# Masks as 32-bit GpSimd products over interleaved row pairs, part of the key writes moved to DMA, eps as a third statistics group, two MLP partial sums in place of three, and a new instruction order

**Chip, cores, metric.** One core of one Trainium2 chip (trn2). The metric is the device time of one execution in microseconds (us); lower is better. Of several runs the median is quoted. The kernel runs on one core, so there is no slower die to compare with; every profiled run of this study is in the fast state, with a mean granted TensorE clock between 0.92 and 1.00.

## The reference

Two identical layers over a 2048 x 512 input: windowed attention, then an MLP that mixes along the sequence. Cut to what matters:

```python
def _A_ref(x, wqkv, wo):                       # B, S, D = 1, 2048, 512
    H = 32; Dh = D // H; W = 256               # 32 heads of 16, window 256
    ...
    scores = jnp.einsum("bhqd,bhkd->bhqk", q, k) * (Dh ** -0.5)
    mask = (idx[:, None] - idx[None, :] >= 0) & (idx[:, None] - idx[None, :] < W)
    p = _softmax(jnp.where(mask[None, None], scores, -1e9), axis=-1)
    ...
def _B_ref(x, w1, b1, w2, b2):                 # F = 1792
    h = _layernorm(x, axis=-1)
    u = _gelu(jnp.einsum("bsd,sf->bdf", h, w1) + b1)
    y = jnp.einsum("bdf,fs->bds", u, w2) + b2
    return y.transpose(0, 2, 1)

for _ in range(2):                             # written out in the original
    x = x + _A_ref(_layernorm(x), A_wqkv, A_wo)
    x = x + _B_ref(_layernorm(x), B_w1, B_b1, B_w2, B_b2)
```

## The kernel before

The kernel first lists all its operations, each with the engines that may run it, and then puts them into the order that a constant, `ORDER`, holds: about 2,500 entries of (next operation, which engine). Every engine runs its own operations in that order and waits on semaphores. So each operation below has a place in an in-order queue, and a change of the place is a change of data, not of code.

Attention works on score units: scores of four head rows for 128 keys and 512 query columns (some have fewer), two PSUM bank pairs, two exps on ScalarE into the bf16 tile `pt`, one or two mask products over the triangular ends of the window, then P V.

```python
for i, ts in enumerate((tA, tB)):
    op("scalar:exp", lambda e, ...: e.activation(
        pt[:, tp.slot, 2 * i:2 * i + 2, 0:cols], pair(ts)[:, :, 0:cols], ACTF.Exp, scale=SMSCALE), ...)
for c0, nc_, w0 in plan[su[0][0]][1]:
    def f_mask(e, ...):
        v = pt[:, tp.slot, :, c0 * 64:c0 * 64 + w]
        msk = ldm[:].rearrange("p a b -> p (a b)")[:, w0 * 64:w0 * 64 + w]
        ...
        return e.tensor_tensor(v, v, msk....to_broadcast([P, 4, w]), op=ALU.mult)
    op("vector:mask", f_mask, ..., alts=[("gpsimd", f_mask, ...)])          # DVE or GpSimd, as the order says
...
# P V reads   rhs=pt[64 * h:64 * h + 64, tp.slot, r, base + c0 * 64:base + (c0 + n) * 64]
```

Keys go through a staging tile into `kbd`, for either half `h` of 16 channels with the other half set to zero, which a product with a 0/1 column (`par`) does:

```python
for h in range(2):
    f_kz = lambda e, h=h: e.tensor_scalar(dst(h), stg[...], par[:, h:h + 1], 0.0, op0=ALU.mult, op1=ALU.add)
    op("gpsimd:kz", f_kz, ..., alts=[("vector", f_kz, ...)])
```

Layer norm takes `bn_stats`, `bn_aggr`, a DVE op for variance plus eps ("var"), a power of -0.5 on GpSimd, and the normalise on DVE. The first MLP product runs in pieces while attention is still going on, and DVE adds each piece to a running sum in SBUF:

```python
PARTS = [[(2, 0, 4), (3, 4, 8), (4, 8, 12)], [(2, 0, 8)]]    # (chunk, first row block, last row block) per layer
```

The softmax here doesn't subtract the row's maximum and nothing guards it: scores larger than these inputs give would overflow.

## Time and profile before

| | kernel before |
|---|---|
| median of 3 runs | 477.62 us (477.6 to 481.74) |
| span of the profiled run, mean granted clock | 476.5 us, 0.988 |
| busy: PE, DVE, ACT, GpSimd (POOL) | 421.0, 368.0, 331.4, 227.6 us |
| first exp starts; last exp of layer 1 and of layer 2 ends | 9.8; 176.0; 394.2 us |
| lengths: attention 1, MLP 1 with attention 2, last MLP | 166.2, 218.2, 82.3 us |

PE is TensorE (PEld its weight loads), DVE VectorE, ACT ScalarE. Busy times say how full an engine is over everything; the three lengths, read off the first and last exp, say where the time goes. The prediction shows the lines behind the table.

### The profile page before, as it was taken

What the parts mean: (1) busy time and instruction counts of PE and PEld (TensorE: products, weight loads), DVE (VectorE), ACT (ScalarE), POOL (GpSimd) and SP (SyncE); (2) the same over time, 40 slices, a digit from 0 to 9 for tenths busy, and PEclk for the clock granted to TensorE, in tenths of its full rate; (3) what the DMA queues carried; (4) which work ended last, traced back from release to release, by engine and by line L of the source; (5) the groups of instructions that cost most, each with busy time, mean ns of one, the idle gap of its engine ahead of it and who ended that gap; (6) DMA issues with size and microseconds to landing.
All of it is one profiled execution on the core that took longest, in us unless ns stands there. A gap on an engine that the chain in (4) does not pass through costs nothing.

```text
span 476.5 us, 14658 instructions
## 1 busy us (share of the span) xinstructions
PE 421.0 (88%) x6355; PEld 199.2 (42%) x6416; DVE 368.0 (77%) x702; ACT 331.4 (70%) x388; POOL 227.6 (48%) x252
## 2 busy tenths in 40 slices
PE   6998887996868688999999998878798999999996
PEld 5855333343323233444554443433333334444442
DVE  7999999989988879726767889998988798630313
ACT  8998988999789780520689989999989992231000
POOL 4677876398477342001046874987755551000000
PEclk9999999999999799999999999999989999999999
DMA  7522604510011317530330310052013136465362
GB/s 220 136 46 62 144 1 36 126 44 3 3 45 34 92 46 227 165 96 11 89 89 14 91 35 3 3 135 46 3 36 89 47 105 183 132 192 142 100 194 71
DMA packets 79392, 39.77 MB, mean 83 GB/s; under 512 B 20960, under 2 KB 79328, under 8 KB 79328
## 3 DMA queue, kind: packets, MB, share of 16 engines
q1 hardware_dynamic: 79328, 38.82, 30.9%
q8 instruction: 51, 0.84, 0.8%
q14 instruction: 13, 0.11, 0.1%
HBM read 33.56 MB, written 2.10 MB: 75 GB/s over the span
## 4 chain that ended last, share of the span: by engine, by line
PE 50%; DVE 30%; ACT 15%; POOL 2%; issue 2%; DMA 0%
PE PS L512 30%; ACT pt L685 14%; DVE pt L695 8%; PE PS L837 7%; PE PS L670 4%; PE PS L607 4%; PE PS L716 4%; DVE rl L736 3%; DVE xh_sb L493 3%; DVE stats L470 2%; DVE x_sb L758 2%; DVE oT L747 1%; DVE vb L618 1%; POOL pt L695 1%; PE PS L514 1%
## 5 line engine op out<-in xcount | busy, mean ns | idle before, releaser
L685 ACT ACTIVATE pt<-PS 128x1024 bf16<-128x1024 f32 (+1 forms) x304 | 283.3, 1043 | 27.1 <-PE PS L670 26.4
L695 POOL TENSOR_TENSOR pt<-pt,ldm 128x256 bf16<-128x256 bf16 (+1 forms) x148 | 147.4, 1006 | 74.3 <-ACT pt L685 62.3
L695 DVE TENSOR_TENSOR pt<-pt,ldm 128x512 bf16<-128x512 bf16 (+1 forms) x124 | 69.7, 569 | 9.1 <-ACT pt L685 7.4
L512 PE MATMUL PS<-xh_sb,w1b 128*128 128x512 bf16 x262 | 69.2, 389 | 7.4 <-issue 2.4
L670 PE MATMUL PS<-qT,kbd 32*128 32x256 bf16 (+4 forms) x1488 | 61.4, 255 | 12.1 <-DVE rl L736 3.6
L512 PE MATMUL PS<-uT,w2b 128*128 128x512 bf16 x268 | 68.4, 379 | 0.9 <-issue 0.6
L486 POOL TENSOR_TENSOR rstd<-rstd,mhalf 128x2 f32<-128x2 f32 (+1 forms) x33 | 23.3, 712 | 78.5 <-DVE rstd L484 77.0
L864 DVE SCALAR_TENSOR_TENSOR x_sb<-PS,b2col,x_sb 128x512 bf16<-128x512 f32 x32 | 23.3, 747 | 47.8 <-PE PS L512 47.7
L716 PE MATMUL PS<-pt,vb 64*32 64x320 bf16 (+4 forms) x2976 | 44.9, 251 | 16.5 <-DVE pt L695 9.0
L512 PE MATMUL PS<-xhT,wqkv 128*128 128x512 bf16 (+1 forms) x218 | 51.6, 364 | 5.3 <-issue 2.2
L670 PEld LDWEIGHTS PS<-qT,kbd 32*128 32x128 bf16 x1488 | 22.1, 93 | 66.9 <-ACT pt L685 40.7
L852 ACT ACTIVATE uT<-rl,b1col 128x512 bf16<-128x512 f32 x28 | 18.3, 712 | 42.5 <-DVE rl L848 42.5
L736 DVE STREAM_TRANSPOSE rl<-PS 128x1024 f32<-128x1024 f32 x32 | 39.7, 1242 | 8.1 <-PE PS L716 7.8
L470 DVE BATCH_NORM_STATS2 stats<-x_sb 128x6 f32<-128x512 bf16 x64 | 42.9, 681 | 3.3 <-DMA x_sb<-in_A_x_dram 2.8
L716 PEld LDWEIGHTS PS<-pt,vb 64*32 64x32 bf16 x2976 | 28.5, 90 | 35.9 <-issue 11.2
L512 PE MATMUL PS<-uT,pt 128*128 128x512 bf16 x165 | 42.2, 379 | 0.2
L512 PEld LDWEIGHTS PS<-xh_sb,w1b 128*128 128x128 bf16 x280 | 23.0, 99 | 39.1 <-issue 11.1
L512 PEld LDWEIGHTS PS<-uT,w2b 128*128 128x128 bf16 x278 | 25.9, 98 | 31.6 <-issue 2.5
L837 PE MATMUL PS<-xh_sb,w1b 128*128 128x512 bf16 x165 | 37.1, 379 | 1.4 <-DVE xh_sb L493 1.2
L493 DVE TENSOR_SCALAR xh_sb<-x_sb,agg,rstd 128x512 bf16<-128x512 bf16 x64 | 34.9, 561 | 2.2 <-POOL rstd L486 2.0
L742 POOL TENSOR_TENSOR ul<-rl,rc 128x512 bf16<-128x512 f32 x23 | 25.8, 1123 | 22.3 <-DVE rc L740 20.5
L607 PE MATMUL PS<-wqkv,xhT 128*64 128x256 bf16 x512 | 34.0, 275 | 1.3 <-DVE rstd L484 1.3
(65 smaller groups left out, 410.3 us busy)
## 6 DMA issues: line engine op xcount, KB each, us to landing
w1b<-in_B_w_dram SPq DMA_DIRECT2D x112, 128.0 KB, 2.7
w2b<-in_B_w_dram SPq DMA_DIRECT2D x70, 128.0 KB, 2.5
pt<-in_B_w_dram SPq DMA_DIRECT2D x42, 128.0 KB, 2.8
out_dram<-x_sb SPq DMA_DIRECT2D x16, 128.0 KB, 2.1
x_sb<-in_A_x_dram SPq DMA_DIRECT2D x3, 512.0 KB, 4.1
wqkv<-in_A_wqkv_dram SPq DMA_DIRECT2D x4, 256.0 KB, 5.1
wqkv<-in_A_wqkv_dram SPq DMA_DIRECT2D x1, 512.0 KB, 6.3
wo_sb<-in_A_wo_dram SPq DMA_DIRECT2D x1, 512.0 KB, 3.8
```

The costliest lines, as they stand in the source:

```text
L470: op("vector:stat", lambda e: e.bn_stats(stats[:, t, :], x_sb[:, t, :]), reads=[f"x{t}"], writes=[f"st{t}"], cost=dve_cost(512), after=lat ...
L486: op("gpsimd:rstd", lambda e: e.tensor_tensor(rstd[:, t0:t1, 0], rstd[:, t0:t1, 0], mhalf[:, 0:1].to_broadcast([P, t1 - t0]), op=ALU.pow), ...
L493: op("vector:xh", lambda e: e.tensor_scalar(xh_sb[:, t, :], x_sb[:, t, :], agg[:, t, 0:1], rstd[:, t, :], op0=ALU.subtract, op1=ALU.mult), ...
L512: return e.matmul(o, lhsT=w, rhs=x, start=start, stop=stop, skip_group_check=True)
L607: last = e.matmul(bank(ft)[64 * j:64 * j + 64, sc * 256:(sc + 1) * 256], lhsT=xhT[:, tx.slot, c, tok:tok + 64], rhs=wqkv[:, c, 1024:1536]. ...
L670: last = e.matmul(bank(tt[r // 2], r % 2)[:, base + c0 * 64:base + (c0 + n) * 64], lhsT=kbd[32 * r:32 * r + 32, tk.slot, o, jj].rearrange( ...
L685: op("scalar:exp", lambda e, ts=ts, tp=tp, i=i, cols=cols: e.activation(pt[:, tp.slot, 2 * i:2 * i + 2, 0:cols], pair(ts)[:, :, 0:cols], A ...
L695: return e.tensor_tensor(v, v, msk.unsqueeze(1).to_broadcast([P, 4, w]), op=ALU.mult)
L716: last = e.matmul(bank(t, h)[32 * r:32 * r + 32, i + q0 * 64:i + (q0 + n) * 64], lhsT=vb[64 * h:64 * h + 64, tk.slot, jj, 4 * o + r, :], r ...
L736: op("vector:od", lambda e, t=tod, tr=tr: e.transpose(rl[:, tr.slot:tr.slot + 2].rearrange("p a b -> p (a b)"), pair(t)), reads=[(tod, i) ...
L742: f_n = lambda e, tr=tr, tl=tl: e.tensor_tensor(ul[:, tl.slot].rearrange("p (q x d) -> p x q d", x=2, d=16), T(tr)[:, :, :, 0:16], R(tl).u ...
L837: last = e.matmul(bank(tu, tt), lhsT=v()[:, sc - b0, k0 + tt * P:k0 + (tt + 1) * P], rhs=xh_sb[:, sc, :], start=(sc == b0), stop=(sc == NT ...
```

## The change

The intent: relieve DVE. Each part takes work from it or from the path that feeds the exps.

1. The probabilities of two score rows are interleaved, so that one int32 holds a pair with the same mask. A mask becomes one GpSimd product over half as many elements; DVE masks are gone.
2. Of 24 key pairs, 14 are written by DMA (eight transfers each) over a `kbd` that was set to zero once.
3. eps enters `bn_aggr` as a third statistics group, so the "var" op goes.
4. The first layer's three partial sums become two.
5. A new order, which also moves some evictions between ACT and DVE.

```diff
-    PARTS = [[(2, 0, 4), (3, 4, 8), (4, 8, 12)], [(2, 0, 8)]]
+    PARTS = [[(2, 0, 4), (4, 4, 12)], [(2, 0, 8)]]
-        ldm = sb("ldm", [P, 4, 64])
+        ldm = sb("ldm", [P, 4, 64], dt.int32)
-        stats = sb("stats", [P, NT, 6], dt.float32)
+        stats = sb("stats", [P, 2, 4, 9], dt.float32)
 ...
+        for i in range(1, 3):
+            op("gpsimd:zk", lambda e, i=i: e.memset(kbd[:, i].bitcast(dt.float32), 0.0), ...)
 ...
+        op("vector", lambda e: e.memset(stats[:, :, :, 6:9], 0.0), writes=["eps0"])
+        for i, c in enumerate((EPS, EPS * EPS / (1.0 + EPS))):
+            op("vector", lambda e, i=i, c=c: e.memset(stats[:, i, :, 8], D * c), ...)
-            op("vector:var", lambda e: e.tensor_scalar(rstd[:, t0:t1, 0], agg[:, t0:t1, 1], a, b, ...), ...)
-            op("gpsimd:rstd", lambda e: e.tensor_tensor(rstd[:, t0:t1, 0], rstd[:, t0:t1, 0], ..., op=ALU.pow), ...)
+            op("gpsimd:rstd", lambda e: e.tensor_tensor(rstd[:, t0:t1, 0], agg[:, t0:t1, 1], ..., op=ALU.pow), ...)
 ...
+        def probs(t):
+            return pt[:, t.slot].rearrange("p a b -> p (a b)").rearrange("p (i c r) -> p i c r", i=2, r=2)
 ...
+                def f_kz(e):
+                    for h in range(2):
+                        for r in range(4):
+                            p = 32 * r + 16 * h
+                            got.append(e.dma_start(kbd[p:p + 16, ...], stg[p:p + 16, ...]))
+                op("sync:kz", f_kz, ..., parts=8, alts=[("gpsimd", f_kz2, 1340), ("vector", f_kz2, ...)])
 ...
-                            pt[:, tp.slot, 2 * i:2 * i + 2, 0:cols], pair(ts)[:, :, 0:cols],
+                            probs(tp)[:, i, 0:cols, :], pair(ts)[:, :, 0:cols].rearrange("p r c -> p c r"),
 ...
+                            v = stepped(probs(tp).bitcast(dt.int32)[:, :, c0:c0 + w, 0], reps, cs)
+                            return e.tensor_tensor(v, v, m, op=ALU.mult)
+                        op("gpsimd:mask", f_mask, ...)
 ...
-                                            rhs=pt[64 * h:64 * h + 64, tp.slot, r, base + c0 * 64:...],
+                                            rhs=probs(tp)[64 * h:64 * h + 64, r // 2, base + c0 * 64:..., r % 2],
```

The rest of the diff is the new `ORDER` constant, a memset of ones over 32-bit words, a merge of two small masks of a unit into one, a factor in the GELU's scale that goes with the third part (`(1.0 + EPS) ** -0.5`, in place of the `1.0 + EPS` in the "var" op), and the bookkeeping of an operation that issues eight transfers.

## The prediction

> **What bounds the kernel now.** I read the page first (busy shares, the 40 slices, the chain by line), then the groups with shapes kept apart, then engine busy time by stage, then the waits of ACT and PE. The page shows no single bound:
>
> ```profile
> PE 421.0 (88%) x6355; PEld 199.2 (42%) x6416; DVE 368.0 (77%) x702; ACT 331.4 (70%) x388; POOL 227.6 (48%) x252
> PE   6998887996868688999999998878798999999996
> DVE  7999999989988879726767889998988798630313
> ACT  8998988999789780520689989999989992231000
> PE 50%; DVE 30%; ACT 15%; POOL 2%; issue 2%; DMA 0%
> ```
>
> The slices show four stages. ACT is high in two blocks, the attention of either layer, and low in two, the two MLPs, where PE alone is at 9. The first and last exp (9.8 and 393 us in the view of their line; in the timeline the first layer's exps stop at 176.0) give the borders, and the busy time of each stage is:
>
> ```profile
> 10.00:176.00 166.00, 137.63 (x2855) 66.68 (x2878) 151.54 (x284) 149.41 (x176) 111.37 (x118) 0.98 0.25 58
> 176.00:248.00 72.00, 69.03 (x528) 33.83 (x517) 50.07 (x105) 25.81 (x36) 10.33 (x14) 1.00 0.42 118
> 248.00:394.00 146.00, 129.29 (x2475) 57.55 (x2497) 127.19 (x236) 136.58 (x152) 99.04 (x106) 0.99 0.21 51
> 394.00:476.50 82.50, 78.26 (x446) 35.55 (x452) 32.56 (x56) 11.85 (x18) 1.79 (x3) 0.99 0.50 144
> ```
>
> Columns after the stretch: PE, PEld, DVE, ACT, POOL, granted clock, DMA share, GB/s. PE is idle only 3.0 and 4.2 us in the MLP stages: they are PE-bound and the change removes no matmul there. In the first attention DVE is 91% busy, ACT 90%, PE 83%; in the second ACT 94%, PE 89%, DVE 87%. So the time to be had is idle time of ACT and PE in the attention stages: ACT 16.6 and 9.4 us, PE 28.4 and 16.7 us. Their waits say why:
>
> ```profile
> ACT pt L685 <- PE PS L670: 26.4, 40, 1.8
> PE PS L716 <- DVE pt L695: 9.0, 13, 2.3
> PE PS L670 <- DVE rl L736: 3.6, 4, 1.1
> ```
>
> ACT's exp waits for scores, in 40 short gaps; PE, in its own order, was held by DVE's mask or by DVE not yet having emptied a PSUM bank. DVE, a fully loaded in-order queue, is the hidden bound of the first attention, ACT close behind.
>
> The parts that the change touches:
>
> ```profile
> L695 POOL TENSOR_TENSOR pt<-pt,ldm 128x512 bf16<-128x512 bf16 x93 | 109.7, 1183 | 50.9 <-ACT pt L685 45.9 <-DVE pt L695 3.3
> L695 DVE TENSOR_TENSOR pt<-pt,ldm 128x512 bf16<-128x512 bf16 x99 | 58.8, 598 | 5.9 <-ACT pt L685 4.2 <-POOL pt L695 1.1
> L695 POOL TENSOR_TENSOR pt<-pt,ldm 128x256 bf16<-128x256 bf16 x55 | 38.6, 707 | 23.4 <-ACT pt L685 16.4 <-DVE pt L695 6.4
> L695 DVE TENSOR_TENSOR pt<-pt,ldm 128x256 bf16<-128x256 bf16 x25 | 11.1, 451 | 3.2 <-ACT pt L685 3.1
> L493 DVE TENSOR_SCALAR xh_sb<-x_sb,agg,rstd x64: 308/406/1319, 5.2 to 407.8; 128x512 bf16<-128x512 bf16 x64
> ```
>
> The last line gives minimum, median and maximum in ns: normalising costs 406 in the median, but 561 in the mean of its group. The tail up to 1319 is not work.
>
> **What the Trainium skill says.** (1) "SBUF — State Buffer", section "Who interferes with whom": GpSimd has only VectorE's second port pair; a VectorE op in a two-port mode, or with two SBUF inputs beside a GpSimd op that reads SBUF, excludes it for the whole instruction. The trace agrees: DVE masks range from 222 to 1845 ns, and at 154.9 us a POOL mask, a DVE mask of 1.41 us and a normalise of 1.14 us follow each other, three times the usual size. (2) "GPSIMD Engine Reference", section 3.1, puts two-input elementwise work at about 2.6 cycles per element, near 2.2 ns. The trace gives (1183 - 707) / 256 = 1.86 ns plus 231 ns fixed, for bf16. That a 32-bit integer multiply costs the same per element no run shows. (3) "SBUF — State Buffer", section "Door 1: The DMA port swizzle", note on cachelines: strides within 16 bytes are free in SBUF (eight bf16), but PSUM lines have 8 bytes and non-contiguous PSUM access slows matmuls. The new layout makes PV read every second bf16 (free by this) and exp read two PSUM banks alternately (not covered; no access of that kind is in the trace). (4) "DMA: Bandwidth & Descriptors", section "Specifications": below 512 B a transfer is not at line rate. The key pieces have 128 B runs, but all kernel loads land in 2 to 3 us here, and the DMA share in attention is 0.25.
>
> **The change, part by part.** The order string is data in the diff; read against the list of operations it has 2,457 entries for 2,531 (33 variance ops, 24 second key halves, 14 partial sums and 8 merged masks fewer, 5 set-up ops more), and it names the engine of each.
>
> Masks: all on POOL, pairs of rows as one int32. Before, 192 masks of 512, 80 of 256, 2 of 1536 and 2 of 512 are 122,880 elements; now 61,440 in 268 ops: 61,440 x 1.86 ns + 268 x 231 ns = 114 + 62 = 176 us on POOL, against 152.5 there before; DVE loses 58.8 + 11.1 + 1.7 = 71.6 us.
> Variance: 33 DVE ops, 7.1 us, go; eps enters the aggregation as a third group. It also takes one hop out of each normalise chain.
> Partial sums: 14 DVE adds of 673 ns, 9.4 us, go. But 56 matmuls (12 us at the 0.216 us between matmuls that the long MLP runs show) leave the fourth chunk's filler for the last one, where PE idled most (clock 0.5 for 6.8 us).
> Keys: of 24 pairs 14 go by DMA, 6 stay on POOL, 4 on DVE: POOL 26.0 to 9.0 us, DVE 6.6 to 4.0 us. Each DMA pair is eight issues on SP, 14 x 8 x 0.47 us = 53 us of a queue that has room.
> Evictions: ACT gives up 6 of q, 2 transposes and 2 of v, takes 1 of k, net 9 x 0.6 = 5 us, nearly all in the first attention; DVE takes them (+5.5 us) and 3 more products (+2.1 us).
> Sums: DVE 368.0 - 71.6 - 7.1 - 9.4 - 2.6 + 5.5 + 2.1 + 1 = 286 us, and up to 64 x 155 ns = 10 us less if the order really avoids the port lock. POOL 227.6 + 23.5 - 17.0 - 3.4 + 2 = 233 us. ACT 331 - 5 = 326 us. PE unchanged.
>
> What lies on the path: only the idle time of ACT and PE in attention. First attention: DVE falls to about 105 of some 152 us, so PE should wait little for it; POOL reaches about 75%. ACT needs 149.4 - 5 = 144.4 us; I let idle fall from 16.6 to 7 us (95% busy, what the second attention nearly has now): 151.5 for 166, saving 14.5. PE would then be 91% busy, above the 89% of the second attention now, so this is near the reach of PE as well. The order leaves 3 more filler ops (6 matmuls, 1.3 us) after the last exp. Second layer: before that layer's first chunk is through its exps, the order has 19 fewer output ops and 12 fewer projection ops (about 13 us of PE); they fill gaps in the next two chunks. Of 16.7 us PE idle I count 7.5 as saved. Sum 14.5 - 1.3 + 7.5 = 20.7 us. Order and chip drift apart, in an in-order queue with a new long POOL stage; I keep 85%: 17.6 us, so 477.6 - 17.6 = 460.
>
> **Rivals.** (a) PE is already the bound: 421 us busy is inflated by waits inside the array, but if it is real work, attention cannot shrink beyond a few us, and the time is 468 to 475. For: PE 83 to 89% there. Against: its idle time is attributed to DVE and ACT. (b) The layout costs: exp over alternating banks or PV at stride 2. 304 exps at 926 ns each back to back are the floor of ACT; 10% more is 28 us and eats everything: 480 to 490. For: nothing in the trace has this access. Against: element and column counts stay. (c) POOL becomes the bound: at the skill's 2.2 ns, or a slower integer multiply, masks take 200 us or more, with normalise roots and products behind them in the same queue; PV then waits for POOL: 468 to 478. (d) SP: eight issues per key pair hold back the weight loads and transposes behind them; PE fillers wait for DMA: 465 to 472. (e) Everything fits and waits vanish: 445 to 450.
>
> **Range and chances.** (a), (c) and (d) each cost part of the gain, (b) all of it. I give (b) about 7%, the other three together a fifth of ending above 468. Range 446 to 474; faster by over 2% (under 468.1) 0.77, within 2% 0.18, slower 0.05.
>
> **What would show it.** Right: masks only on POOL, 268, near 0.4 to 0.7 us each, 160 to 185 us in sum; DVE near 280; normalise mean close to 0.4 us; exp unchanged at 1.05 us mean, 926 ns apart; first-layer exps done near 162 instead of 176; MLP stages as long as before. Wrong: exp or PV durations up (b); PE or its weight loads waiting for POOL masks (c) or for a key or weight DMA (d); or ACT waiting for scores as long as before while DVE is now idle (a), which would mean that DVE was never what held PE.

## The result, and the profile after

The changed kernel takes 460.86 us (median of 4 runs, 458.47 to 462.53), the kernel before in the same comparison 478.77 us (4 runs, 477.6 to 481.74). Ratios here are the mean time of one kernel's fast runs over that of the other's of the same rounds, so not quite the ratio of the medians: 0.961, 95% interval 0.955 to 0.968.

The page's busy line, three of its slice lines and the chain by engine, after:

```profile
PE 429.6 (94%) x6392; PEld 200.0 (44%) x6392; DVE 296.9 (65%) x540; ACT 327.2 (71%) x379; POOL 234.3 (51%) x345
PE   6798889899797999999999998999999999999997
DVE  7896768766696569645657684778776377530234
ACT  5997979999999870533988988999999990250000
PE 55%; ACT 21%; POOL 13%; DVE 4%; DMA 2%; SPq 2%; issue 2%; POOLq 0%
```

DVE went from 368.0 to 296.9 us and from 30% of the chain that ends last (the last instruction, followed back to whatever released each step) to 4%. GpSimd took its place in the chain, 2% to 13%, though it is busy only 51% of the time.

The stages after, cut at the same events as before (last exp of layer 1 at 168.7, of layer 2 at 376.5); the columns are the stretch, its length, busy PE, PEld, DVE, ACT, POOL, granted clock, DMA share and GB/s. The cut inside the middle part is at 230.0 here and 248.0 before, so only the first and the last line are stage against stage:

```profile
10.00:168.70 158.70, 141.79 (x2833) 66.91 (x2832) 115.39 (x215) 147.01 (x171) 112.80 (x162) 0.98 0.28 64
168.70:230.00 61.30, 61.30 (x483) 29.03 (x481) 40.91 (x79) 27.36 (x37) 9.97 (x16) 1.00 0.41 114
230.00:376.50 146.50, 141.09 (x2572) 63.05 (x2572) 101.69 (x175) 136.32 (x154) 102.43 (x151) 1.00 0.29 66
376.50:459.20 82.70, 79.45 (x457) 35.70 (x454) 31.93 (x53) 11.54 (x17) 2.93 (x5) 1.00 0.52 150
```

The first line lost 7.3 us, the last one nothing (82.7 against 82.5). The two lines between them together lost 10.2 us (218.0 to 207.8). PE's busy time in the first attention reads 4.2 us more than before, but that is no more work: of the matmuls of that stretch 23 have no record in the first trace (2855 beside 2878 weight loads) and none is missing in the second. The changed kernel profiled again (run 12), with 22 missing, reads 138.2 us in the same stretch. Compared with about as many missing on both sides, PE's idle time there fell from 28.4 to 20.5 us.

The groups of masks, exps and normalises after, shapes kept apart (busy, mean ns of one, then idle time before), and the spread of the normalise:

```profile
L722 POOL TENSOR_TENSOR pt<-pt,ldm 128x256 int32<-128x256 int32 x202 | 147.9, 741 | 59.6 <-ACT pt L704 54.2
L722 POOL TENSOR_TENSOR pt<-pt,ldm 128x128 int32<-128x128 int32 x64 | 29.6, 466 | 26.9 <-ACT pt L704 26.0
L704 ACT ACTIVATE pt<-PS 128x1024 bf16<-128x1024 f32 x292 | 275.4, 1051 | 22.6 <-PE PS L689 21.6
L498 DVE TENSOR_SCALAR xh_sb<-x_sb,agg,rstd x64: 315/411/1862, 5.3 to 391.0; 128x512 bf16<-128x512 bf16 x64
```

An int32 mask costs (741 - 466) / 128 = 2.15 ns per element and 191 ns fixed. The exp has not changed (before: 1054 ns), although it now reads two PSUM banks by turns. The normalise has the same median (411 against 406) and a tail as long as before; the mean in its group is 522 against 561 ns (541 in run 12, the same kernel again).

The waits that matter, after (what waits, for what: us in total, times, longest). In the kernel before, line L704 was L685, L689 was L670, L738 was L716:

```profile
POOL pt L722 <- ACT pt L704: 82.5, 64, 8.7
ACT pt L704 <- PE PS L689: 21.6, 35, 2.1
PEld PS L738 <- POOL pt L722: 16.4, 28, 1.4
PE PS L738 <- POOL pt L722: 7.2, 17, 1.1
```

ACT's wait for scores fell only from 26.4 to 21.6 us. The waits of PE for DVE's masks are gone; in their place P V (L738) waits for GpSimd's masks, 16.4 us at the weight load and 7.2 us at the matmul.

### The profile page after: what moved, and what is told of

It reads as the page before. It is cut to its first block, busy times and chain, and to the rows that moved or that the text cites. A ratio compares the mean times of both kernels' runs of the same rounds, so it can differ in the third digit from the quotient of the medians.

```text
span 459.2 us, 14685 instructions
## 1 busy us (share of the span) xinstructions
PE 429.6 (94%) x6392; PEld 200.0 (44%) x6392; DVE 296.9 (65%) x540; ACT 327.2 (71%) x379; POOL 234.3 (51%) x345
## 3 DMA queue, kind: packets, MB, share of 16 engines
q1 hardware_dynamic: 98528, 40.67, 34.6%
## 4 chain that ended last, share of the span: by engine, by line
PE 55%; ACT 21%; POOL 13%; DVE 4%; DMA 2%; SPq 2%; issue 2%; POOLq 0%
PE PS L520 34%; ACT pt L704 20%; POOL pt L722 11%; PE PS L859 8%; PE PS L689 5%; PE PS L738 5%; PE PS L626 2%; DMA xhT<-xh_sb 2%; DVE rl L758 1%; PE PS L522 1%; SPq L606 1%; DVE xh_sb L498 1%; POOL ul L764 1%; ACT kbd L588 1%; SPq L549 1%
## 5 line engine op out<-in xcount | busy, mean ns | idle before, releaser
L704 ACT ACTIVATE pt<-PS 128x1024 bf16<-128x1024 f32 (+1 forms) x304 | 282.8, 1040 | 22.6 <-PE PS L689 21.6
L722 POOL TENSOR_TENSOR pt<-pt,ldm 128x256 int32<-128x256 int32 (+1 forms) x268 | 179.0, 683 | 88.7 <-ACT pt L704 82.5
L520 PE MATMUL PS<-xh_sb,w1b 128*128 128x512 bf16 x280 | 69.7, 381 | 1.4 <-DVE xh_sb L498 0.7
L689 PE MATMUL PS<-qT,kbd 32*128 32x256 bf16 (+4 forms) x1488 | 61.5, 253 | 7.9 <-ACT pt L704 2.2
L520 PE MATMUL PS<-uT,w2b 128*128 128x512 bf16 x272 | 65.9, 380 | 0.0
L520 PE MATMUL PS<-xhT,wqkv 128*128 128x512 bf16 (+1 forms) x266 | 63.0, 363 | 2.2 <-DMA xhT<-xh_sb 1.3
L738 PE MATMUL PS<-pt,vb 64*32 64x320 bf16 (+4 forms) x2976 | 45.6, 253 | 8.0 <-POOL pt L722 7.2
L491 POOL TENSOR_TENSOR rstd<-agg,mhalf 128x2 f32<-128x2 f32 (+1 forms) x33 | 22.9, 701 | 57.5 <-DVE agg L480 53.0
L689 PEld LDWEIGHTS PS<-qT,kbd 32*128 32x128 bf16 x1488 | 22.3, 93 | 63.6 <-ACT pt L704 47.5
L738 PEld LDWEIGHTS PS<-pt,vb 64*32 64x32 bf16 x2976 | 28.7, 89 | 27.5 <-POOL pt L722 16.4
L498 DVE TENSOR_SCALAR xh_sb<-x_sb,agg,rstd 128x512 bf16<-128x512 bf16 x64 | 32.2, 522 | 11.7 <-POOL rstd L491 11.7
L520 PE MATMUL PS<-uT,pt 128*128 128x512 bf16 x168 | 39.5, 379 | 0.0
L520 PEld LDWEIGHTS PS<-uT,w2b 128*128 128x128 bf16 x272 | 24.9, 98 | 31.0 <-issue 3.8
L520 PEld LDWEIGHTS PS<-xh_sb,w1b 128*128 128x128 bf16 x280 | 23.4, 98 | 33.4 <-issue 7.2
L626 PE MATMUL PS<-wqkv,xhT 128*64 128x256 bf16 x512 | 35.1, 280 | 0.9 <-DVE rl L758 0.5
L520 PEld LDWEIGHTS PS<-xhT,wqkv 128*128 128x128 bf16 x266 | 22.1, 98 | 28.5 <-issue 7.1
L520 PE MATMUL PS<-wo_sb,oT 128*128 128x512 bf16 x122 | 30.8, 380 | 0.5 <-ACT pt L704 0.4
## 6 DMA issues: line engine op xcount, KB each, us to landing
x_sb<-in_A_x_dram SPq DMA_DIRECT2D x3, 512.0 KB, 7.4
wqkv<-in_A_wqkv_dram SPq DMA_DIRECT2D x1, 512.0 KB, 7.7
```

Source lines behind the costliest of these rows:

```text
L491: op("gpsimd:rstd", lambda e: e.tensor_tensor(rstd[:, t0:t1, 0], agg[:, t0:t1, 1], mhalf[:, 0:1].to_broadcast([P, t1 - t0]), op=ALU.pow), ...
L498: op("vector:xh", lambda e: e.tensor_scalar(xh_sb[:, t, :], x_sb[:, t, :], agg[:, t, 0:1], rstd[:, t, :], op0=ALU.subtract, op1=ALU.mult), ...
L520: return e.matmul(o, lhsT=w, rhs=x, start=start, stop=stop, skip_group_check=True)
L626: last = e.matmul(bank(ft)[64 * j:64 * j + 64, sc * 256:(sc + 1) * 256], lhsT=xhT[:, tx.slot, c, tok:tok + 64], rhs=wqkv[:, c, 1024:1536]. ...
L689: last = e.matmul(bank(tt[r // 2], r % 2)[:, base + c0 * 64:base + (c0 + n) * 64], lhsT=kbd[32 * r:32 * r + 32, tk.slot, o, jj].rearrange( ...
L704: op("scalar:exp", lambda e, ts=ts, tp=tp, i=i, cols=cols: e.activation(probs(tp)[:, i, 0:cols, :], pair(ts)[:, :, 0:cols].rearrange("p r ...
```

## Experiments

There were twelve runs. Runs 1, 2, 4 and 7 shared one chip, with 479.3 us as the median of the kernel before; 3, 6, 8 and 10 another (479.85 us), 5, 9, 11 and 12 a third (479.24 us). Parts 3 (eps) and the moved evictions were not tested on their own. "Starts/ends" gives the first exp, and the ends of the last exp of layer 1 and layer 2, then the span of the profiled run.

### 1. Only DVE's mask work taken from the kernel before

Is DVE the hidden bound? Every mask that the order gives to DVE touches two columns, all instructions and waits stay. Its output is wrong, which doesn't matter for the time.

```diff
                         def f_mask(e, ...):
+                            if e is nc.vector:
+                                v = pt[:, tp.slot, :, c0 * 64:c0 * 64 + 2]
+                                return e.tensor_tensor(v, v, ldm[:, 0, 0:2].unsqueeze(1).to_broadcast([P, 4, 2]), op=ALU.mult)
```

> The kernel before, its order untouched, but the 126 masks that VectorE does cover 2 columns instead of 256 to 1536 elements (wrong result on purpose): VectorE loses about 50 us of work and of port conflicts, nothing else changes. My theory (VectorE was the hidden bound of attention): even with the old order the time falls by 2 to 4%, to 460 to 468 us, and the exps of the first layer end by 168 us instead of 176. Rival 1 (the new order is what pays, load matters little): within 1% of before, 473 to 479 us. Rival 2 (TensorE itself is the bound): also within 1%.

Measured: 468.64 us, ratio 0.976 (0.970 to 0.982). Starts/ends 9.9 / 170.4 / 384.5 / 466.6. DVE is busy 338.0 us, and ACT's wait for scores is down to

```profile
ACT pt L685 <- PE PS L670: 17.8, 34, 1.5
```

and the tiny masks' own line is

```profile
L694 DVE TENSOR_TENSOR pt<-pt,ldm 128x8 bf16<-128x8 bf16 x126 | 40.6, 327 | 14.2 <-ACT pt L685 12.0 <-POOL pt L698 1.3
```

So DVE's mask time was on the path: 30 us less of it gave 10.7 us. That is over half of the whole gain, without a mask having gone anywhere else. The expectation was missed a little: I had counted on 50 us less DVE time, exps of layer 1 done by 168 and 468 us at most. The same tiny instruction took 95 to 1583 ns (median 166), so a good part of its 40.6 us can't be work; point (1) of the prediction would blame the shared port, which this run does not test. And the run takes three things away at once: DVE's load, what those masks did to GpSimd (busy 221.6 in place of 227.6 us), and P V's waits for them (9.0 and 4.7 us before, 4.1 and 2.8 here).

### 2. Only the masks moved to GpSimd, in the old order

The int32 layout and masks from the change, all on GpSimd, each at the place where the old order had it; nothing else.

```diff
-                        op("vector:mask", f_mask, ..., alts=[("gpsimd", f_mask, 100 + 2.03 * nm)])
+                        op("gpsimd:mask", f_mask, ...)        # int32, exp and P V over interleaved pairs
```

> The kernel before with the pair layout and all masks as int32 on GpSimd, everything else and the order as before. GpSimd goes to about 250 us, VectorE to about 295 us. My theory (relief of VectorE pays by itself): half or more of the gain, 462 to 471 us. Rival 1 (order): 474 to 482 us, as the order was made for masks on two engines. Rival 3 (a longer queue on GpSimd takes back what VectorE gives): waits of TensorE for masks on GpSimd rise from 5 to over 30 us and the time is 475 us or more.

Measured: 512.01 us, ratio 1.066 (1.058 to 1.074). Starts/ends 9.8 / 197.7 / 428.5 / 512.5. The waits:

```profile
POOL pt L698 <- ACT pt L680: 101.7, 67, 4.8
ACT pt L680 <- PE PS L665: 58.0, 51, 3.8
PEld PS L714 <- POOL pt L698: 50.1, 34, 3.4
PE PS L714 <- POOL pt L698: 38.0, 24, 2.9
```

GpSimd is busy 251.7 us, 49% of the span, and yet P V waits 88 us for it, while it waits itself 101.7 us for exps. My theory fell, and the sign of rival 3 is there. But an engine that is half idle and waited for at once may also stand behind the wrong thing in its queue, and run 3 tests that. In the old order, neighbouring masks often stood on different engines, so it did not matter that a later unit's mask came before an earlier one's; put together in one queue, 96 of 276 masks stand behind a mask of a later score unit. In the changed kernel 56 of 268 do.

### 3. The same with the masks in unit order

As 2, but GpSimd's masks are exchanged among their places so that they follow the order of the score units; 193 of 276 move, nothing else does.

> The kernel of b_masks (512 us), with the masks in GpSimd's queue put into the order of the score units that they belong to; the places that masks take in the order stay, only which mask stands at which place changes (193 of 276 move). In b_masks 96 masks stand behind a mask of a later unit, since the old order had interleaved two engines. Theory: this blocking at the head of the queue (the mask in front waits for an exp that comes later) is most of the loss of 33 us: 475 to 490 us, TensorE's waits for masks on GpSimd under half of b_masks. Rival: a mask pair simply takes longer one after the other on one engine than side by side on two, and the old order leaves too little room for that: 500 to 515 us.

Measured: 475.54 us, ratio 0.991 (0.988 to 0.993). Starts/ends 11.5 / 170.4 / 390.3 / 473.0.

```profile
POOL pt L698 <- ACT pt L680: 49.7, 68, 2.4
PEld PS L714 <- POOL pt L698: 24.0, 28, 2.5
ACT pt L680 <- PE PS L665: 21.9, 33, 1.4
```

The place in the queue alone is worth 36 us. Moving the masks then pays 0.9%: less than the 2.4% of run 1. GpSimd is no free place: P V waits 38 us for its masks (24.0 here and 14.4 at the matmul).

### 4. All operations of the change in the old order

As the changed kernel, with three partial sums kept and the order of the kernel before; operations that have gone are taken out of it. (The ring of statistics has 8 in place of 4, since the old order needs more at a time.)

> All operations of the change except the two partial sums (three as before), each at the place in the order that its counterpart had before; keys on the engines that the change picks; the statistics ring is 8 deep instead of 4 as the old order needs it. Rival 1 (order pays): 472 to 482 us, so the order is worth over half of the 3.9%. My theory: 462 to 470 us. If it is slower than the masks alone, keys by DMA with eight issues each hurt in an order that was not made for them.

Measured: 515.54 us, ratio 1.072 (1.065 to 1.080). P V waits 47.4 and 34.6 us for masks, as in 2: my theory fell here too, and run 5 mends the queue.

### 5. The same with the masks in unit order

187 masks exchanged.

> All operations of the change except the two partial sums, in the order of before with every mask put into unit order in GpSimd's queue. Theory (the old order lost only by masks of a later unit standing ahead of those of an earlier one; the operations then pay by themselves): 464 to 470 us, exps of the first layer done near 169. Rival (the new schedule as a whole, not only the place of the masks, is what turned the operations into time): 474 us or more, no better than the masks alone in unit order (475.5).

Measured: 479.61 us, ratio 1.002 (0.998 to 1.006). My theory fell: with the queue mended, the operations of the change in the old order give nothing, 1.1% less than the masks alone. Starts/ends 15.0 / 173.5 / 399.1 / 481.3. Against the other kernels:

| kernel | first exp | its exps, layer 1 | from there to the first exp of layer 2 | its exps, layer 2 | last MLP |
|---|---|---|---|---|---|
| before | 9.8 | 166.2 | 59.3 | 159.0 | 82.3 |
| masks alone, sorted (3) | 11.5 | 158.9 | 59.9 | 160.0 | 82.7 |
| all operations, sorted (5) | 15.0 | 158.5 | 59.6 | 166.0 | 82.2 |
| changed kernel | 11.2 | 157.5 | 47.2 | 160.6 | 82.7 |

(All in us; layer 2's first exp starts at 235.23, 230.29, 233.12 and 215.82. The profiled run of 5 was the slowest of its four, 483.04 us against a median of 479.61, so some of its losses here may be that run's alone. The first exp of the changed kernel started at 12.4 us in run 12, so a difference of 1 us is within the spread.) The first attention is as short as in the changed kernel, once its exps have started. So the operations do pay there, and the new order is worth little in it. The losses are at the start (5.2 us later than before) and in layer 2's exps (166.0), and what the changed kernel gains in the second layer, run 5 lacks altogether: every kernel in the old order, whatever its operations, needs 59 to 61 us from the last exp of layer 1 to the first of layer 2, and the changed one 47. What was taken out of that stretch can be read from `ORDER`, decoded as the kernel does it: TensorE has 46 ops of the second MLP product between these two exps in place of 70, 4 ops of projections in place of 12, and 14 of the partial sums of the first product in place of 11. The trace agrees: 147 weight loads on the line of the plain large matmuls (L520) in place of 194 (L512). One place of the loss in layer 2's exps, in the chain of waits that ended last (start, duration, what):

```profile
270.74 0.81 DVE xh_sb L493
...
271.57 1.23 SPq L544
...
272.86 0.60 SPq L601
...
277.36 1.36 SPq L601
...
278.77 1.28 SPq L544
...
280.09 2.53 DMA xhT<-xh_sb
...
282.66 0.39 PE PS L515
```

Between the two transposes (L544) SyncE issues the eight transfers of one key pair (L601), 5.9 us, and PE waits for the second transpose. This is rival (d) of the prediction, come true in the old order; in the changed kernel SyncE has 2% of that chain, against 4% here.

### 6. The changed kernel with bf16 masks

Is it the 32-bit pair that makes GpSimd masks affordable? Same order, same places, but the product runs over the same bytes as bf16, twice the elements.

```diff
-        ldm = sb("ldm", [P, 4, 64], dt.int32)
+        ldm = sb("ldm", [P, 4, 64, 2])
-                            v = stepped(probs(tp).bitcast(dt.int32)[:, :, c0:c0 + w, 0], reps, cs)
+                            v = stepped(pt[:, tp.slot]...[:, :, 2 * c0:2 * (c0 + w)], reps, 2 * cs)
```

> The changed kernel with the same masks on GpSimd as bf16 products over twice the elements, same places in memory and in the order. A 512-element mask should take 1.15 us instead of 0.73, so GpSimd gets some 110 us more, 345 us in all and nearly all of the attention stages: 500 to 540 us. If it stays under 480 us, GpSimd's load is not what matters and the 32-bit form is not needed. It also measures the cost per element of both types in one setting.

Measured: 544.13 us, ratio 1.136 (1.132 to 1.139).

```profile
L723 POOL TENSOR_TENSOR pt<-pt,ldm 128x512 bf16<-128x512 bf16 x202 | 232.5, 1164 | 46.7 <-ACT pt L704 41.6
L723 POOL TENSOR_TENSOR pt<-pt,ldm 128x256 bf16<-128x256 bf16 x64 | 43.6, 684 | 21.0 <-ACT pt L704 20.1
```

GpSimd is busy 334.7 us and the bound (41% of the chain). A mask of a full unit takes 1164 against 741 ns: 1.88 ns per element in bf16, 2.15 in int32, but half as many. Without the pairs this change, in this order, would be a heavy loss.

### 7. The changed kernel with the keys back on GpSimd

The 14 key pairs that go by DMA run on GpSimd, at the same places in the order. Only the order's data change.

> The changed kernel, with the 14 key pairs that go by DMA put on GpSimd instead (2 x 14 ops of about 0.73 us, 20 us more of GpSimd; SP loses 112 issues of 0.6 us). If GpSimd is now the short engine in attention (its masks are 11% of the chain), it costs 1 to 2%: 464 to 470 us. If keys by DMA are neutral because they lie off the path: within 0.5%, 459 to 463 us. If the SP issues held up loads and transposes: faster, under 458 us.

Measured: 466.95 us, ratio 0.973 (0.968 to 0.978), against 0.961 to 0.964 for the changed kernel: the keys by DMA are worth about 1% in this order. GpSimd is busy 252.9 us and has 20% of the chain. Starts/ends 12.5 / 168.7 / 382.2 / 465.5: all of the loss is in the second layer. The page's line of these issues, from the changed kernel:

```profile
kbd<-stg SPq DMA_DIRECT2D x112, 16.0 KB, 2.0
```

Each lands 2.0 us (median) after its issue, and each issue holds SyncE for 600 ns (median).

### 8. Three partial sums in the changed kernel

The second sum (rows 4 to 12) is cut in two again, in place: 14 more DVE adds of about 0.7 us, no matmul more.

```diff
+                    for h0, h1 in [(s0, s1)] if s1 - s0 != 8 or s0 == 0 else [(s0, s0 + 4), (s0 + 4, s1)]:
                         ...
+                            op("vector:evu" if h1 == s1 else "vector:evx", lambda e, ...: e.tensor_tensor(dst, bank(ft), dst, op=ALU.add), ...)
```

> The changed kernel with the large partial sum of the first layer (rows 4 to 12) cut into two accumulations again, in place: 14 more adds of 0.68 us on VectorE in the last chunk, no other order. My theory (VectorE is no longer the bound): within 0.5%, 459 to 463 us. Rival: PSUM banks come free later and hold up TensorE: 464 to 470 us.

Measured: 479.64 us, ratio 0.999 (0.997 to 1.002): the whole gain gone, where I had expected next to nothing. Starts/ends 12.4 / 182.0 / 395.5 / 478.2. Both the theory and the rival (470 us at most) were missed. PE now waits for these adds, 21.6 us in the four largest groups, where in the changed kernel no such wait adds up to more than 0.7 us:

```profile
PEld PS L514 <- DVE w2b L846: 7.2, 7, 1.5
PEld PS L514 <- DVE uT L846: 6.9, 8, 1.3
PE PS L514 <- DVE w2b L846: 4.4, 7, 1.1
PE PS L514 <- DVE uT L846: 3.1, 4, 0.8
```

Two things changed at once: 10 us more DVE work, and 14 more PSUM banks that a matmul group holds until DVE has read them. Run 9 parts them.

### 9. The DVE time of those adds without the bank

14 `bn_stats` of 0.68 us on DVE at the places of the adds, into a spare tile that nobody reads.

```diff
+                        if s1 - s0 == 8:
+                            op("vector:load", lambda e, i=(f0 + k) // P: e.bn_stats(spare[:, i, :], x_sb[:, s0, :]), ...)
```

> The changed kernel with 14 extra bn_stats of about 0.68 us each on DVE, at the places where the three-sum kernel had its 14 extra adds, but holding no PSUM bank and waited for by nobody. Theory (the three-sum kernel lost 19 us because TensorE waited for a PSUM bank that DVE frees late, not by DVE's time): within 1% of the changed kernel, 458 to 465 us. Rival (10 us more DVE work in the last chunk is itself the loss, by pushing back DVE's masks and evictions): 470 us or more.

Measured: 462.05 us, ratio 0.964 (0.961 to 0.967); the changed kernel in the same rounds 461.73 us, 0.964 (run 12). So the DVE time costs nothing at these places: in the changed kernel DVE is no bound there any more. What run 8 lost comes, by elimination and by its own waits, from the accumulations that hold a bank for DVE. That run put them into an order laid out for two sums, so its 19 us are no measure of what the fourth part of the change is worth; an order made for three sums could hide some. One bound follows all the same: even so, layer 2's first exp comes 53.3 us after layer 1's last one (235.31 - 182.00), 6 us sooner than before. So about half of the 12 us by which the new order starts layer 2 sooner doesn't hang on the two sums. The ops that TensorE has in that stretch are the same as in the changed kernel (decoded as in 5); there the adds still run until 202, and PE is busy 49.0 of the 53.3 us, while in the changed kernel it is busy all the 47.2.

### 10. The changed kernel with its masks in unit order

139 of the 268 masks exchanged among their places in GpSimd's queue.

> The changed kernel with its masks on GpSimd put into the order of their units in the same way (139 of 268 move; 56 stood behind one of a later unit). If blocking at the head of the queue is what is left of GpSimd on the chain: 452 to 458 us. Rival: the order was made knowing its one queue, the inversions are there for a reason: 459 to 464 us, or worse.

Measured (6 runs): 458.43 us, ratio 0.957 (0.953 to 0.960). Starts/ends 12.5 / 166.7 / 373.5 / 456.1. That is between what I expected (452 to 458) and the rival (459 to 464). ACT's wait for scores is 17.7 us, P V's waits for masks 12.9 and 5.0.

### 11 and 12. The same with one zero fill moved, and the changed kernel again

At the start of the changed kernel GpSimd clears the key tile (a memset, which only writes) beside the second normalise. The timeline of the changed kernel, lines of these two tiles (start, duration):

```profile
5.28 0.37 DVE L498 TENSOR_SCALAR xh_sb<-x_sb,agg,rstd 128x512 bf16<-128x512 bf16 x1
6.02 1.80 POOL L460 MEMSET kbd<- 128x2048 f32 x1
6.11 1.86 DVE L498 TENSOR_SCALAR xh_sb<-x_sb,agg,rstd 128x512 bf16<-128x512 bf16 x1 [0.46 <-POOL rstd L491]
```

The second normalise starts 0.09 us after the memset and ends 0.15 us after it, as if it stood still meanwhile. Run 11 moves the fill behind the third power, on top of 10; run 12 is the changed kernel unaltered, in the same rounds.

> The changed kernel with masks in unit order and GpSimd's second zero fill moved behind its third rstd, so that it no longer stands beside the second normalise. If the 1.4 us that the second normalise lost beside the fill are on the path of the start: 456 to 457.5 us (the sorted kernel had 458.4). If the first scores wait for something else: 458 to 459, as the sorted kernel.

> The changed kernel again, unaltered, as the measure of the other three on this chip: 458.5 to 462.5 us, ratio to before 0.955 to 0.968.

Measured: run 11 458.41 us (6 runs), ratio 0.958 (0.954 to 0.961); run 12 461.73 us (5 runs), ratio 0.964 (0.962 to 0.966). Without the fill beside it the normalise is short, in the timeline of run 11 (run 10, with the fill where it was, has 1.86 us too):

```profile
5.28 0.37 DVE L492 TENSOR_SCALAR xh_sb<-x_sb,agg,rstd 128x512 bf16<-128x512 bf16 x1
6.10 0.41 DVE L492 TENSOR_SCALAR xh_sb<-x_sb,agg,rstd 128x512 bf16<-128x512 bf16 x1 [0.46 <-POOL rstd L485]
```

1.86 us became 0.41, but the time stayed where 10 had it. The first exp starts at 11.2 us here, at 11.2 to 12.6 in the other runs built on the changed kernel, so a gain of 1.4 us at the start could not be seen beside that spread. In run 12's rounds the mean of run 11 is 0.6% less than that of the changed kernel (458.58 against 461.35 us; single runs overlap, 455.27 to 461.18 and 460.22 to 462.32): unit order, with or without the fill moved, is the fastest version that I have, by a little.

## Why the prediction was right, and where its steps were not

The total was right: 460.0 predicted, 460.86 measured, and the class too. By its steps:

- **"The time to be had is idle time of ACT and PE in the attention stages."** Right. The last MLP did not move, and the gain lies in the stretch up to the last exp of layer 2.
- **"DVE ... is the hidden bound of the first attention."** Right, and shown by run 1, 30 us less of mask time on DVE, 10.7 us less in all, 5.6 of them by the end of the first attention; how much of it is DVE's load and how much the lock or the wait of P V for a mask, that run leaves open. Run 9 shows the other side: 14 ops of 0.68 us put on DVE after the change cost nothing.
- **Masks, 176 us on GpSimd in 268 ops.** 179.0 measured (the group on the page, 268 ops). The error is in the rate: 2.15 ns per element and 191 ns fixed in place of 1.86 and 231, which nearly cancel.
- **DVE to 286 us, "and up to 64 x 155 ns = 10 us less if the order really avoids the port lock".** DVE is at 296.9, and two steps are behind that. The sum took busy times of groups off the busy time of the engine, but neighbours overlap in the record: the groups, shapes kept apart, sum to 402.8 us before for 368.0 busy, and to 318.8 after for 296.9. So the groups lost 84.0 us, about the 82 that the prediction took off, but the engine 71.1. And the lock step failed: normalise still reaches 1862 ns, and the mean of 522 gives 2.5 us in place of 10. The long normalises are still there, whatever the order's intent; at the start it even puts a new GpSimd memset beside a normalise. Run 11 shows that this instance costs 1.45 us of DVE and no time that could be seen.
- **GpSimd to 233, ACT to 326 us.** 234.3 and 327.2.
- **Key issues, 0.47 us each, "of a queue that has room".** 600 ns, so 112 x 0.6 = 67 us. The room is there in the new order, and not in the old one (run 5: 5.9 us of issues between two transposes, on the chain).
- **First attention saves 14.5 - 1.3 us.** Too much: 7.3 by its end. The terms that were mis-sized are ACT's idle time, taken as 7 us after the change (over the first stage ACT is idle 158.7 - 147.0 = 11.7 us), and its work, taken as 144.4 us and measured as 147.0: of the evictions that it gave up only 2.4 us show in this stage. Its waits for scores fell only from 26.4 to 21.6 us overall. GpSimd's masks stand between exp and P V now, and P V waits for them 23.6 us. Run 10 shows that part of this is the masks' order: sorted, 17.9 us of it are left, and the last exp of layer 1 comes 1.9 us sooner (166.7). And the start is later: the first exp came at 11.2 in place of 9.8 us.
- **Second layer saves 7.5 us.** Too little: 10.4 (218.2 to 207.8). The prediction read in the order that about 13 us of PE work would no longer stand before layer 2's exps, and that fits: ACT starts them 12.1 us sooner (47.2 us after the last exp of layer 1 in place of 59.3; run 5 has the ops). But it counted a gain of 7.5, on the view that the work moved would fill gaps only in part. The exps of layer 2 took 160.6 us in place of 159.0, so 10.4 of the 12.1 us stayed. The gain of the second layer is this earlier start and nothing else.
- **The factor of 0.85** stood for what order and chip lose to each other. No run measures it; 20.7 times 0.85 hit the 17.7 us of the two stretches (7.3 and 10.4) because a term too large and one too small came together. That the total was so near is luck in this.
- **Readings that were off.** The idle times of PE (28.4 and 16.7 us, 3.0 and 4.2 in the MLPs) count matmuls without a record as idle. "All kernel loads land in 2 to 3 us" holds for the MLP weights (2.5 to 2.8); most of those of the set-up took 3.6 to 6.3. Exps back to back start 904 ns apart (median, before and after), not 926. The first fed the 7.5 us of the second layer, which were taken as a part of the 16.7; the other two carry nothing.
- **Rivals.** (a) did not happen as put: the time is under its 468 to 475 us. But PE has the largest share of the chain (55%), and is busy all of the 47.2 us between the layers' exps. (b) did not happen: exp 1051 against 1054 ns, and the P V matmul over every second element takes 300 against 298 ns in its largest group. (c) is what bounds the changed kernel in part, by place more than by load: 13% of the chain at 51% busy; with the keys on GpSimd it has 20% (run 7), and with bf16 masks it becomes the bound (run 6). (d) happens in the old order (run 5). (e) did not: ACT still waits 21.6 us for scores.
- **What I had not thought of:** that the masks could not have been moved in the old order. Run 2 lost 6.6%. I had read the order as a means of the change, and it is a part of it without which the other parts give nothing (run 5). Its worth is the earlier start of layer 2's exps. Whether an order with three sums could start them as soon is not settled: run 8, in an order made for two, gives half of it back in waits for the adds.

## What to carry to other kernels

When work that two engines shared is gathered on one in-order engine, put its instructions into the order in which they are needed before judging the move: here that alone turned a loss of 6.6% into a gain of 0.9%. An engine that is half idle and waited for can be a sign of the wrong order in its queue rather than of too much work; try the order first. It is not all of it: with its masks in unit order GpSimd is busy 52% and P V still waits 17.9 us for it (run 10). And taking time from a loaded engine is best tested by making its instructions tiny in place: a wrong result, but one run that says whether the engine is on the path, as long as one looks at how long the tiny instructions really took.

## What the Trainium skill lacked or had wrong

- "SBUF — State Buffer", section "Who interferes with whom": nothing wrong found; the number is what it lacks. It names the normalise's kind (`tensor_scalar`) as one that can contend with GpSimd in a two-port mode, and runs 10 and 11 agree, beside a GpSimd memset that only writes: 1.86 us beside it, 0.41 without.
- "GPSIMD Engine Reference", section 3.1: near 2.2 ns per element for two-input work fits int32 products (2.15 ns), and not bf16 ones (1.86 to 1.88 ns). It has no figure by type, and no word on packing two bf16 into an int32 to multiply by 0 or 1 (the skill reads bf16 as int32 for VectorE copies only): 741 in place of 1164 ns for the same bytes. The outputs are right. That the product is exact for every pair no run shows.
- "Perfetto Trace Analysis", section "Tensor Engine Instruction": it calls GpSimd a strict FIFO, which these runs bear out. It doesn't say how to see it in a trace, nor its size: 512.0 against 475.5 us for the same instructions in another order within one queue.
- "DMA: Bandwidth & Descriptors": it splits up the fixed time of a transfer, but I found no figure for how long an issue holds SyncE's queue. Here it is 600 ns (median of 112), and eight in a row held a transpose behind them for 5.9 us.
- No page covers an exp that reads two PSUM banks by turns: 1051 ns against 1054 with each bank read through.
